# Four transformer layers on one core: the third layer's sliding-block units gathered into two runs of four, and into one run of eight for the last chunk

## The chip, the core and the metric

The kernel runs on one core of one Trainium2 chip. The metric is the device time of one execution in microseconds (us). A core has five engines that run side by side and meet through semaphores: TensorE (PE in the profile, its weight loads PEld) multiplies matrices, ScalarE (ACT) computes exponentials, VectorE (DVE) and GpSimd (POOL) do elementwise work, and SyncE (SP) issues DMA transfers. ACT, POOL and SP also have a queue of their own for issuing transfers; what stands in a queue is issued in order.

## The reference: what is computed

The input x has 2048 rows of 640 numbers. Four attention layers follow one another, and each adds its result to x:

```python
x = A_x
x = x + _A_ref(_layernorm(x, axis=-1), A_wqkv, A_wo)
x = x + _B_ref(_layernorm(x, axis=-1), B_wqkv, B_wo)
x = x + _A_ref(_layernorm(x, axis=-1), A_wqkv, A_wo)
x = x + _B_ref(_layernorm(x, axis=-1), B_wqkv, B_wo)
```

Both kinds have 32 heads of 20 numbers: queries, keys and values come from one product with wqkv, scores are q·k/sqrt(20), softmax over the keys, the weighted sum of the values, and a product with wo. In `_A_ref` a query sees itself and the 255 keys before it (a sliding block); in `_B_ref` it sees all 2048 keys. The kernel numbers the layers 0 to 3, so that 0 and 2 are sliding ("windowed" in the code) and 1 and 3 are full. The change concerns layer 2, the third layer.

## The kernel before

**Chunks, groups, units.** The rows are cut into 4 chunks of 512 queries and the heads into 8 groups of 4. The attention of one layer, one chunk and one group is a *unit*, `Unit(l, c, g)`; below it is written l.c.g. A full unit has 64 *banks* (16 blocks of 128 keys by 4 heads; one bank is a 128 x 512 block of scores in PSUM), a windowed unit has 12. Layer 3's chunk 0 is done in two parts, over key blocks 0 to 11 (48 banks) and, later, 12 to 15 (16 banks), because its last keys are ready late.

**Tiles.** The banks of all units stand in one list in the order of `units` and are cut into *tiles* of three banks (some of two). For each tile PE computes the scores (line 1316, two halves of three or four of the eight PSUM banks), ACT takes the exponential of the whole tile in one instruction (line 1347, into a tile `pt` of 6 buffers), and two or three tiles later PE multiplies by the values (line 1380). A tile of a windowed unit is masked in between: `affine_select` on POOL (line 1419) and a product with a mask on DVE (line 1429); its product with the values waits for both. In a full unit of layer 1 two of the 64 banks are "aside": their exponential is made on DVE (line 918 and following), and their scores sit in two tiles whose ACT instruction has two banks. So a layer-1 unit of chunk 1 to 3 has 21 or 22 tiles, a windowed unit 4, and a first part in layer 3 has 16.

**Background work.** The chain between two layers has to go on while these tiles run: when all 8 units of (l, c) have ended and been divided by their softmax sums (the *tails*, lines 1020 to 1090, one for two units that ended one after the other, about 8 tiles long), the output projection `t_out` is queued (work 9.0), and with it, for the same chunk of the next layer, the layer norm `t_ln` (1.6), the values `t_v` (5.6) and ten blocks `t_block` of 128 features, one for keys and one for queries (1.1 each; `qk`, line 536 stores the block to DRAM, line 337 loads its weights, both from the POOL queue). A windowed unit g then loads its rows of q and k from DRAM on the SP queue (lines 770 and 771). Each of these tasks uses a bank of PSUM, number 6, that all of them share.

**Due times set the pace.** A task is due when the first unit that needs it starts. Between two tiles `pump` gives the background an amount `rate(t)`:

```python
        def rate(t):
...
            done, r = 0.0, 0.6 if state["early"] else 0.3
            for task in todo:
                done += max(task.left, 0.0)
                if task.need < len(units):
                    r = max(r, done / max(starts[id(units[task.need])] - t - 16, 1))
            return min(1.1 * r, 1.0 if u.l == 0 else 0.9)
```

`starts` holds the tile with which a unit starts; the work is meant to be over 16 tiles ahead, the amount per tile is at least 0.33 and at most 0.9, and what isn't done when the unit starts is done there and then (`require`). If a tile has little background work, `keep_clock` adds matmuls whose result nobody reads (`unread`, in the profile `ps<-masks,ident`), so that PE stays busy.

**Where the change is.** The order of `units` is written out by hand. Behind each unit g of layer 1's chunk c (c = 1, 2, 3), and for c = 4 behind each first part of layer 3's chunk 0, a tuple says how many of layer 2's eight units of chunk c - 1 follow. Before, they stand in pairs behind the units g = 2, 3, 4 and 5, and for the last chunk two, three and three behind g = 2, 3 and 4. The starts by tile follow from the bank counts: 2.0.0 starts at tile 413, 2.1.0 at 616, 2.2.0 at 819, 2.3.0 at 1005; the last units of the four chunks end at tiles 509, 712, 915 and 1069. Layer 3's first parts start at tile 957, its second parts at 1117, and layer 3's chunk 1 at 1160.

Of the kernel before, what the change touches and what calls it, by code (L numbers as in the profile page):

```python
# [26 lines left out]
NC = S // C  # L27
# [21 lines left out]
def kernel(  # L49
# [689 lines left out]
    for c in range(1, NC + 1):  # L739
        small = deque(Unit(2, c - 1, g) for g in range(G))  # L740
        for g in range(G):
            units.append(Unit(1, c, g) if c < NC else Unit(3, 0, g, PARTS[3][0]))
            for _ in range(((0, 0, 2, 2, 2, 2, 0, 0) if c < NC else (0, 0, 2, 3, 3, 0, 0, 0))[g]):
                units.append(small.popleft())
    units += [Unit(3, 0, g, PARTS[3][1]) for g in range(G)]
    units += [Unit(3, c, g) for c in range(1, NC) for g in range(G)]
# [730 lines left out]
```

## Time and profile before

| | |
|---|---|
| median of 3 runs | 2251.73 us (2251.3 to 2252.52) |
| the profiled execution | 2252.22 us, its span 2250.5 us |
| ACT busy | 2147.6 us, 95% of the span, 1734 instructions |
| of these line 1347, the exponentials | 2110.4 us, 1656 instructions |
| PE busy | 1959.8 us (87%) |
| DVE busy | 1201.6 us (53%) |
| POOL busy | 485.4 us (22%) |
| granted TensorE clock, mean | 0.989 |

The profiled execution took 1.7 us more than its span (start and end, outside the trace) and 0.5 us more than the median of the runs. In the profile "L1347" is line 1347 of the kernel, `pt<-ps` an instruction that reads the tile `ps` and writes `pt`, and a time behind "<-" is idle time of an engine and what ended it. A stretch A:B of the trace runs from A to B us after the span's start. Some positions, read from the starts of ACT's exponentials: tile 349 (unit 1.1.0) at 493.0 us, 413 at 580.6, 552 (unit 1.2.0) at 755.8, 616 at 845.2, 755 (unit 1.3.0) at 1030.9, 819 at 1124.1, 957 at 1310.8, 1005 at 1383.4, 1117 at 1537.6, 1160 at 1595.1.

### The profile page before, as it was taken

To read this page: it belongs to the slowest core of one execution; us is meant where nothing else is said; L and a number is where in the kernel's file an instruction comes from. 1 tells how busy PE (TensorE), PEld (TensorE's weight loads), DVE (VectorE), ACT (ScalarE), POOL (GpSimd) and SP (SyncE) were. 2 spreads that over 40 slices of the span, in tenths; PEclk is the share of its full clock that TensorE was granted. 3 is DMA by queue.
4 is the path that set the end of the run, shared out by engine and by line. 5 is a ranking of instruction groups with operands and counts; after the bars stand their busy time and mean duration, and the time that the engine had idled before them with its cause. 6 is when DMAs were issued, how large, how long until landed. Compare 5 with 4: busy or idle time off the path is not lost.

```text
span 2250.5 us, 71088 instructions
## 1 busy us (share of the span) xinstructions
PE 1959.8 (87%) x30915; PEld 773.2 (34%) x30915; DVE 1201.6 (53%) x2178; ACT 2147.6 (95%) x1734; POOL 485.4 (22%) x950
## 2 busy tenths in 40 slices
PE   8989899988888888888888888888888888888888
PEld 4444443334333343333333443343332222222222
DVE  6656564435343554345453533242567767767774
ACT  7899899999999999999899999999999999999997
POOL 6664544201111124111331123212000000000000
PEclk9999999999999999999999999999999999999999
DMA  6233322422110233012320033103111111111100
GB/s 197 73 98 89 92 79 86 106 71 65 58 35 21 62 100 89 15 35 58 95 84 15 23 105 105 29 22 92 58 59 31 31 34 40 31 31 37 43 25 16
DMA packets 88408, 137.15 MB, mean 61 GB/s; under 512 B 20766, under 2 KB 63486, under 8 KB 88094
## 3 DMA queue, kind: packets, MB, share of 16 engines
q1 hardware_dynamic: 68878, 79.43, 12.7%
q0 software_dynamic: 19216, 53.17, 8.1%
q8 instruction: 242, 3.96, 0.7%
q14 instruction: 72, 0.59, 0.1%
HBM read 99.52 MB, written 27.79 MB: 57 GB/s over the span
## 4 chain that ended last, share of the span: by engine, by line
ACT 47%; PE 26%; issue 16%; DVE 9%; POOL 1%; DMA 1%; SPq 1%; ACTq 0%; DVEq 0%; POOLq 0%
ACT pt L1347 46%; PE ps L300 16%; PE ps L1316 6%; PE ps L1380 2%; DVE st L323 1%; DVE x_sb L568 1%; DVE on L1090 1%; DVE va L323 1%; DVE pt L1429 1%; PE ps L1086 1%; DVE vs L323 0%; DVE raw_o L934 0%; PE ps L437 0%; DVE xnT L323 0%; SPq L1103 0%
## 5 line engine op out<-in xcount | busy, mean ns | idle before, releaser
L1347 ACT ACTIVATE pt<-ps 128x1536 bf16<-128x1536 f32 (+2 forms) x1656 | 2110.4, 1448 | 70.4 <-PE ps L1316 58.0
L300 PE MATMUL ps<-masks,ident 128*32 128x512 bf16 x6344 | 549.7, 390 | 101.3 <-ACT pt L1347 58.2
L1316 PE MATMUL ps<-qt,kt 32*128 32x512 bf16 x3960 | 549.5, 386 | 88.8 <-ACT pt L1347 80.6
L1380 PE MATMUL ps<-pt,vt 128*21 128x512 bf16 x3904 | 397.9, 383 | 0.3 <-ACT pt L1347 0.2
L1316 PEld LDWEIGHTS <-kt 32*128 32x128 bf16 x3960 | 163.7, 91 | 551.2 <-issue 536.4
L1419 POOL TENSOR_SCALAR_AFFINE_SELECT pt<-pt 128x256 bf16<-128x256 bf16 (+2 forms) x505 | 215.8, 448 | 376.5 <-ACT pt L1347 339.4
L300 PEld LDWEIGHTS <-ident 128*32 128x32 bf16 x6344 | 165.5, 94 | 342.6 <-issue 332.0
L300 PE MATMUL ps<-xnT,wqk 128*32 128x512 bf16 x3320 | 221.6, 384 | 16.4 <-DVE st L323 7.9
L1429 DVE TENSOR_TENSOR pt<-pt,masks 128x512 bf16<-128x512 bf16 (+4 forms) x267 | 114.0, 439 | 190.0 <-ACT pt L1347 188.2
L323 DVE CAST st<-ps 128x512 bf16<-128x512 f32 x134 | 92.7, 692 | 210.8 <-PE ps L300 210.7
L300 PE MATMUL ps<-wop,on 128*32 128x320 bf16 x3712 | 157.7, 302 | 17.1 <-DMA on<-on 6.3
L918 DVE TENSOR_SCALAR xnT<-ps 128x512 int32<-128x512 f32 x136 | 93.6, 688 | 134.7 <-PE ps L912 123.6
L1380 PEld LDWEIGHTS <-vt 128*21 128x21 bf16 x3912 | 105.6, 91 | 129.2 <-issue 90.7
L1316 PE MATMUL ps<-qa,ka 32*128 32x384 bf16 (+2 forms) x1408 | 118.7, 278 | 32.2 <-ACT pt L1347 29.6
L300 PEld LDWEIGHTS <-on 128*32 128x32 bf16 x5760 | 116.8, 95 | 80.6 <-issue 58.3
L568 DVE TENSOR_TENSOR x_sb<-x_sb,ps 128x320 bf16<-128x320 bf16 x120 | 58.3, 486 | 125.0 <-PE ps L300 124.7
L1090 DVE TENSOR_TENSOR on<-on,ps 128x512 bf16<-128x512 bf16 x128 | 86.4, 684 | 68.6 <-PE ps L1086 66.6
L300 PE MATMUL ps<-wv,xnT 128*32 128x320 bf16 x2560 | 112.5, 301 | 10.2 <-DVE on L1090 2.2
L300 PEld LDWEIGHTS <-wqk 128*32 128x32 bf16 x3320 | 79.9, 96 | 111.6 <-issue 58.8
L864 DVE CAST on<-ps 128x512 bf16<-128x512 f32 x112 | 77.0, 688 | 69.9 <-PE ps L1389 38.1
L934 DVE SCALAR_TENSOR_TENSOR xnT<-xnT 128x1024 f32<-128x1024 f32 x68 | 83.3, 1225 | 2.3
L1316 PEld LDWEIGHTS <-ka 32*128 32x128 bf16 x1408 | 43.6, 92 | 116.3 <-issue 109.1
(100 smaller groups left out, 1468.2 us busy)
## 6 DMA issues: line engine op xcount, KB each, us to landing
vt<-v_d SPq DMA_DIRECT2D x48, 336.0 KB
kt<-k_d SPq DMA_DIRECT2D x192, 80.0 KB
wqk<-in_B_wqkv_dram POOLq DMA_DIRECT2D x80, 160.0 KB, 3.5
wqk<-in_A_wqkv_dram POOLq DMA_DIRECT2D x70, 160.0 KB, 3.5
k_d<-st POOLq DMA_DIRECT2D x75, 128.0 KB, 2.4
q_d<-st POOLq DMA_DIRECT2D x75, 128.0 KB, 2.3
qt<-q_d SPq DMA_DIRECT2D x384, 20.0 KB
v_d<-vs POOLq DMA_DIRECT2D x16, 336.0 KB, 3.5
```

Of the source, the lines that this page charges most:

```text
L300: nc.tensor.matmul(out_[r], lhsT=lhsT[:, r], rhs=rhs, start=start, stop=stop)
L323: nc.vector.tensor_copy(out=out_, in_=in_)
L568: nc.vector.tensor_tensor(out=xv, in0=had, in1=yp, op=ALU.add)
L864: nc.vector.tensor_copy(out=oT, in_=op)
L918: V.tensor_scalar(out=xi.bitcast(I32)[:, i * C : (i + 1) * C], in0=side["psum"], scalar1=SCALE * LOG2E * FIX, scalar2=-127.0 * FIX, op0=AL ...
L934: V.scalar_tensor_tensor(out=xi, in0=xm, scalar=EA, in1=xm, op0=ALU.add, op1=ALU.mult)
L1090: nc.vector.tensor_tensor(out=oT, in0=oT, in1=zb, op=ALU.mult)
L1316: nc.tensor.matmul(sp[:, i, col * P : (col + qn) * P], lhsT=u.k(kc, j), rhs=u.q(j, q0, qn), start=True, stop=True,)
L1347: nc.scalar.activation(out=pt[:, i:k, b0 * P :], in_=sp[:, i:k, b0 * P :], func=ACT.Exp, scale=SCALE,)
L1380: nc.tensor.matmul(op[32 * j : 32 * j + VW, q0 * P : (q0 + qn) * P], lhsT=u.v(kc, j), rhs=pg[:, i, col * P : (col + qn) * P], start=(first ...
L1419: nc.gpsimd.affine_select(out=v, in_=v, compare_op=ALU.is_gt if later else ALU.is_ge, fill=0.0, base=0, pattern=[[0, k - i], [-1 if later ...
L1429: nc.vector.tensor_tensor(out=pt_[:, i:k, cols], in0=pt_[:, i:k, cols], in1=mv_, op=ALU.mult)
```

## The change

One line changes. In chunks c = 1 to 3 the eight units of layer 2 come as four behind unit 1.c.3 and four behind 1.c.4; in the last, all eight behind the first part of 3.0.3. Nothing is added to or taken from the units themselves.

```diff
         for g in range(G):
             units.append(Unit(1, c, g) if c < NC else Unit(3, 0, g, PARTS[3][0]))
-            for _ in range(((0, 0, 2, 2, 2, 2, 0, 0) if c < NC else (0, 0, 2, 3, 3, 0, 0, 0))[g]):
+            for _ in range(((0, 0, 0, 4, 4, 0, 0, 0) if c < NC else (0, 0, 0, 8, 0, 0, 0, 0))[g]):
                 units.append(small.popleft())
```

With the same bank counts the starts become: 2.0.0 at tile 435, 2.1.0 at 637, 2.2.0 at 840, 2.3.0 at 1021; the last windowed units end at tiles 488, 691, 893 and 1053. Every other landmark stays (552, 755, 957, 1117, 1160).

## The prediction

> **What bounds the kernel.** I read the page first, then the waits of ACT, then ACT's exponentials by stretch.
>
> ```profile
> PE 1959.8 (87%) x30915; PEld 773.2 (34%) x30915; DVE 1201.6 (53%) x2178; ACT 2147.6 (95%) x1734; POOL 485.4 (22%) x950
> ...
> L1347 ACT ACTIVATE pt<-ps 128x1536 bf16<-128x1536 f32 (+2 forms) x1656 | 2110.4, 1448 | 70.4 <-PE ps L1316 58.0
> ```
>
> ACT is the bound, and its exponentials are 2110 of its 2148 us; when it idles, it is for PE's scores (58.0 of 70.4 us). The change leaves every exponential as it is: with the bank counts I get 1161 tiles up to unit 3.1.0 and the same number of ACT instructions in both orders, and 240 selects and 128 mask products for layer 2 in both. So only the waiting can change. Where it stands, the stretches show (us, ACT busy and instructions, granted clock, DMA share, GB/s):
>
> ```profile
> 493.00:580.60 87.60, 85.05 (x65) 1.00 0.28 73
> 755.80:857.90 102.10, 96.44 (x74) 0.99 0.29 83
> 1030.90:1124.10 93.20, 85.77 (x66) 0.98 0.25 72
> 1250.60:1310.80 60.20, 56.75 (x44) 1.00 0.21 56
> 1310.80:1383.40 72.60, 66.85 (x50) 1.00 0.37 100
> 1469.00:1537.60 68.60, 65.52 (x50) 1.00 0.20 53
> 1124.10:1250.60 126.50, 126.29 (x97) 1.00 0.15 46
> 1383.40:1469.00 85.60, 85.60 (x66) 1.00 0.16 48
> 1415.30:1431.20 15.90, 15.90 (x13) 1.00 0.22 61
> ```
>
> The last row is twelve tiles of three consecutive windowed units without a gap: 15.9/12 = 1.33 us a tile, the bare pitch. Successive starts of two-bank tiles without a wait are 0.90 us apart. A stretch is *late* by its length less 1.33 and 0.90 for each of its tiles (busy time hides part of this, since a record of ACT gets longer when the next instruction isn't there):
>
> - A, 493.0 (tiles 349 to 413, before layer 2's chunk 0): 58 x 1.33 + 6 x 0.90 = 82.5; late 5.1
> - B, 755.8 (552 to 624, before and into chunk 1): 93.2; late 8.9
> - C, 1030.9 (755 to 819, before chunk 2): 82.5; late 10.7
> - D, 1250.6 (915 to 957, from chunk 2's last unit to layer 3): 54.1; late 6.1
> - E, 1310.8 (957 to 1005, before chunk 3): 63.8; late 8.8
> - F, 1469.0 (1069 to 1117, from chunk 3's last unit to the second parts): 63.8; late 4.8
> - the calm stretches between, 1124.1 and 1383.4: late 1.4 and 0.5.
>
> Together 44 us, and all of it lies just before a due time. The tasks' own rows say why (projection matmuls of `wqk` in C, before the due time, and in a calm stretch as long as one unit):
>
> ```profile
> 1086.80:1124.10 37.30, 15.73 (x224) 6.24 (x224) 0.00 (x0) 7.32 (x9) 0.95 0.34 105
> 1134.70:1162.00 27.30, 7.63 (x104) 2.38 (x104) 0.00 (x0) 2.59 (x3) 1.00 0.23 68
> ```
>
> The first has 224 of them in 22 tiles and is late by 8.9 us; the second 104 in 21 tiles and late by 0.2. Ten a tile make PE late with the scores, five fit.
>
> **The change, part by part.** *More time before the due times.* The work due with the first windowed unit is 9.0 + 1.6 + 5.6 + 2.2 = 18.4. The projection that starts it (`ps<-wop,on`) begins at 506.8, 773.6, 1048.5, 1264.7, 1328.8 and 1485.1 us: tiles 359, 565, 768, 925, 970 and 1080. By `rate` that is, as 1.1 x 18.4/(due - start - 16), with due tile before and after:
>
> - A: 413, then 435: 0.53 to 0.34
> - B: 616, then 637: 0.58 to 0.36
> - C: 819, then 840: 0.58 to 0.38
> - D: due 957 in both, but the last unit ends 22 tiles earlier; it now makes a tail of its own, some 5 tiles, so start 905 or so: 0.9 (the cap) to 0.56
> - E: 1005, then 1021: 0.9 to 0.58
> - F: due 1117, start 16 tiles earlier, 1064: 0.9 to 0.55
>
> A rate of 0.36 is the calm stretch's (floor 0.33). What is late at 0.58 B and C show: through output projection and layer norm 1.3 and 1.8 us; only behind that, when the 16 tiles of margin are used up and the rate climbs to 0.9, 7.5 and 8.9. So I take for after: A 3.0 (bursts of the layer norm and of the start, 1.8, stay), B 1.5, C 1.8 (calm level), D 2.0 (of its blocks only b = 0 is due at 957, the next 16 tiles later), E 4.5 (the output projection's 3.5 go to 0.6, its blocks stay like B's), F 1.7. Saved: 2.1 + 7.4 + 8.9 + 4.1 + 4.3 + 3.1 = 29.9 us. Bounds: nothing (if a burst is as large at any rate) and 37 (all at the calm level, some 1.2 each).
>
> *Longer runs of windowed tiles.* Runs grow from 8 and 12 tiles to 16 and 32. The load of one such tile shows in the twelve of 1415.3:
>
> ```profile
> 850.50:857.90 7.40, 5.86 (x82) 1.95 (x74) 4.38 (x7) 5.74 (x6) 6.77 (x14) 0.80 0.65 185
> ...
> 1104.10:1107.50 3.40, 3.40 (x31) 1.12 (x34) 1.02 (x2) 1.43 (x1) 0.03 (x1) 0.50 0.00 0
> 1415.30:1431.20 15.90, 12.34 (x215) 5.09 (x214) 6.47 (x13) 15.90 (x13) 9.60 (x20) 1.00 0.22 61
> ```
>
> (columns: PE, PEld, DVE, ACT, POOL busy). POOL is busy 60%, DVE 41%, PE 78%, and no time is lost. But 850.5, unit 2.1.1, shows what happens when a block falls among them: POOL issues two weight loads (1.73 us) and a store (0.56) ahead of the selects, PE waits for masks, ACT for PE, and four tiles take 7.35 instead of 5.32, 2.03 us late (part of it at a halved clock, below). A block costs POOL 0.87 + 0.57 = 1.44 us. In A to C the blocks are now over before the run or nearly; in E those due at tiles 1033 to 1045 (three pairs) can fall into the run. I take two such incidents, 4.1 us; ends: none (as at 1415.3), and one in each unit that has windowed units before it in its run, 6 x 3 + 7 = 25, 51 us.
>
> *Loads and queues.* SP issues 8 loads for each windowed unit, some 0.3 us each, 2.4 us in 5.3; four units can be ahead (`QA`), so the fifth is loaded three units, 16 us, before its use; POOL's stores land 2.3 us after issue. Waits of PE on these transfers are 4 us in all now. I cost it at nothing; if this cover went, the price is of the size of those 4 us. *One tail more* in each of c = 1 to 3 (an odd unit): 16 tiny matmuls and some 0.35 + 0.21 + 0.20 + 0.21 us on DVE, beside a DVE at half load: nothing. The unread matmuls fill whatever tasks leave, so PE's total hardly moves.
>
> *The clock.* At 1104.1 and 854.9 the granted clock was 0.50 for 3.4 us; twenty matmuls took 2.33 us there, 1.29 elsewhere, and the tile at 1104.1 came 2.1 us late. The twelve windowed tiles kept 1.00. I add nothing. The Trainium skill ("TensorE: Matmul & The Clock Gate", "HAM oscillation — how this bites in real kernels") speaks against long thin stretches: idle gaps of PE over about 3.4 us halve its clock. By that rule, once in each of the seven runs at the 2.1 us seen, the sum would be 15 us worse, 2241; the trace shows no such gap in a run. The skill also has POOL and DVE share SBUF interfaces when DVE reads two SBUF inputs ("GPSIMD Engine Reference", "Specifications"), as the masks do; but the same pairs meet in both orders.
>
> **Sum.** 2252.2 (the profiled execution) - 29.9 + 4.1 = 2226.4; its 0.5 us over the median I subtract: 2226.
>
> **Rivals.**
> 1. *The late due times gain nothing*: D, E and F go from the cap to 0.56, near B's rate, and B is as late as E. Then 18.4 us (A to C) are saved, 4.1 lost: 2238. Against it: in D to F half of the loss stands at the output projection, which at B's rate cost 1.3. Chance 0.16.
> 2. *All becomes calm* and the runs cost nothing: 2252 - 37 = 2215. Against it: E's rate isn't calm. Chance 0.11.
> 3. *The work only moves*: the same bursts, bound to the one shared bank and not to the pace, stand in other tiles: 2252. Against it: the 104 matmuls of the calm stretch. Chance 0.06.
> 4. *Slower: POOL in the runs.* Masks, stores and weight loads share one in-order queue; if tasks (layer 3's too) keep running in the runs and each of the 25 units is late as 2.1.1 was: 2252 - 30 + 51 = 2273. It decides from 15 such units on. For it: 850.5; against: 1415.3, and that the work is over sooner. Chance 0.05.
>
> My forecast, 2226 (2217 to 2236), gets 0.62. The range 2214 to 2241 takes in rivals 1 and 2 to their own small spread and leaves out 3 and 4. A measurement of this kernel can tell about 0.2%, 4.5 us, from no change: faster 0.62 + 0.16 + 0.11 = 0.89, same 0.06, slower 0.05.
>
> **What would show it.** Right: stretches B and C fall to 1 to 2 us late, D and F lose their bursts of 28 and more `wop` matmuls a tile, ACT's wait for scores falls from 58 us to some 42 (the six stretches hold 28 us of ACT's idle time for their 44 us of lateness), windowed runs keep 1.33. Wrong: "ACT waits for POOL" (4.4 us now) grows; the blocks of `wqk` still come ten a tile before tiles 637 and 840; halved clocks inside the runs.

## The result, and the profile after

The changed kernel takes 2230.31 us (median of 4 runs, 2229.77 to 2231.19), the kernel before 2252.12 in the same comparison: ratio 0.9906, 95% interval 0.9894 to 0.9918, that is 21 us or 0.94% faster. 2226 was forecast, range 2214 to 2241. The profiled execution took 2229.77 us, its span 2228.1.

The page's line of the exponentials, then the rows of ACT's waits for scores and for masks:

```profile
L1347 ACT ACTIVATE pt<-ps 128x1536 bf16<-128x1536 f32 (+2 forms) x1656 | 2104.2, 1456 | 55.4 <-PE ps L1316 45.7
```

```profile
ACT pt L1347 <- PE ps L1316: 45.7, 71, 3.2
...
ACT pt L1347 <- POOL pt L1419: 2.7, 2, 2.2
```

Still 1656 exponentials; ACT waits 45.7 us for scores in place of 58.0 (42 was forecast), and less for POOL than before (2.7, was 4.4). The same six stretches, found again from the starts of ACT's exponentials (us, ACT busy and instructions, clock, DMA share, GB/s):

```profile
494.20:578.20 84.00, 83.73 (x66) 1.00 0.19 48
755.50:850.00 94.50, 93.94 (x74) 1.00 0.29 79
1024.20:1109.50 85.30, 84.44 (x66) 1.00 0.25 69
1240.60:1298.80 58.20, 55.01 (x44) 0.97 0.26 73
1298.80:1363.70 64.90, 64.89 (x49) 1.00 0.26 72
1451.60:1516.40 64.80, 64.39 (x49) 1.00 0.26 71
```

A comes down from 87.6 to 84.0 us, B from 102.1 to 94.5, C from 93.2 to 85.3, D from 60.2 to 58.2, E from 72.6 to 64.9 and F from 68.6 to 64.8. As lateness (length less 1.33 us for each tile of three banks and 0.90 for each of two), in the kernels that are compared most below:

| | A | B | C | D | E | F | A to F | 624-755 | 819-915 | 1005-1069 |
|---|---|---|---|---|---|---|---|---|---|---|
| before | 5.1 | 8.9 | 10.7 | 6.0 | 8.7 | 4.7 | 44.1 | 3.1 | 1.4 | 0.5 |
| after | 1.4 | 2.2 | 2.7 | 4.1 | 1.1 | 1.0 | 12.5 | 3.5 | 6.0 | 2.7 |
| late start only | 1.4 | 4.7 | 1.5 | 6.8 | 2.1 | 4.7 | 21.3 | 4.7 | 6.3 | 2.4 |
| early end only | 6.4 | 5.6 | 9.0 | 3.4 | 6.3 | 0.2 | 30.9 | 2.5 | 3.3 | 1.6 |
| after, old pace | 6.8 | 4.8 | 9.4 | 4.5 | 5.4 | 2.7 | 33.6 | 2.1 | 4.8 | 2.6 |
| before, no margin | 0.9 | 22.8 | 10.5 | 11.2 | 8.6 | 6.5 | 60.5 | 3.4 | 14.5 | 11.1 |
| before, margin of 8 | 1.8 | 5.5 | 6.2 | 7.6 | 8.3 | 6.2 | 35.6 | 3.5 | 2.6 | 0.3 |
| one run of eight | 1.1 | 4.0 | 3.3 | 0.4 | 1.1 | 0.3 | 10.1 | 2.2 | 2.2 | 2.7 |

The last three columns are the calm stretches between, named by their tiles. The six stretches give 31.6 us. What comes back is 9: 4.6 us in tiles 819 to 915, 2.2 in 1005 to 1069, 2.1 in tiles 413 to 552 (the stretch with chunk 0's windowed units, not in the table) and 0.4 in 624 to 755; 1.9 us more are lost ahead of tile 349, where both kernels are the same. Seven profiled kernels of this study have the same code up to that tile, and it took them 474.9 to 481.0 us from the first exponential on: a single profile's total is good to a few us only, so totals below are medians and single stretches are read from profiles. One execution of the study, the first of the late start below, took 8681 us and is left out: its matmuls took about four times as long (the unread ones 1543 ns in the mean, 390 before) at a recorded clock of 1.00, while the exponentials took 1362 ns (1448 before).

The tasks answer to the rows of the prediction (projection matmuls of `wqk` just before chunk 2's due tile; columns PE, PEld, DVE, POOL busy):

```profile
1080.00:1109.50 29.50, 2.17 (x36) 0.69 (x28) 0.00 (x0) 2.29 (x3) 1.00 0.20 57
...
1109.50:1138.50 29.00, 10.36 (x144) 3.15 (x140) 0.00 (x0) 5.20 (x6) 1.00 0.41 119
```

36 of these matmuls stand in the 22 tiles of unit 1.3.2 where 224 stood before; 144 stand in the unit behind it (second row), at some seven a tile, and that unit is 0.6 us late. Unit 1.3.2 took 37.3 us and takes 29.5.

### The profile page after: what moved, and what is told of

Its sections match the earlier page's. It is cut to its first block, busy times and chain, and to the rows that moved or that the text cites. A ratio compares the mean times of both kernels' runs of the same rounds, so it can differ in the third digit from the quotient of the medians.

```text
span 2228.1 us, 70079 instructions
## 1 busy us (share of the span) xinstructions
PE 1933.2 (87%) x30410; PEld 757.7 (34%) x30411; DVE 1200.5 (54%) x2190; ACT 2141.2 (96%) x1734; POOL 484.0 (22%) x950
## 3 DMA queue, kind: packets, MB, share of 16 engines
q1 hardware_dynamic: 68878, 79.43, 12.8%
## 4 chain that ended last, share of the span: by engine, by line
ACT 51%; PE 22%; issue 17%; DVE 7%; DMA 1%; POOL 1%; SPq 0%; ACTq 0%; DVEq 0%; POOLq 0%
ACT pt L1347 50%; PE ps L300 13%; PE ps L1316 6%; PE ps L1380 2%; DVE on L1090 1%; DVE st L323 1%; DVE pt L1429 1%; DMA wqk<-in_B_wqkv_dram 1%; PE ps L1086 1%; PE ps L437 0%; DVE x_sb L568 0%; DVE on L864 0%; SPq L1103 0%; DVE raw_o L918 0%; DVE xnT L323 0%
## 5 line engine op out<-in xcount | busy, mean ns | idle before, releaser
L1347 ACT ACTIVATE pt<-ps 128x1536 bf16<-128x1536 f32 (+2 forms) x1656 | 2104.2, 1456 | 55.4 <-PE ps L1316 45.7
L300 PE MATMUL ps<-masks,ident 128*32 128x512 bf16 x5840 | 513.8, 389 | 118.3 <-ACT pt L1347 68.4
L1429 DVE TENSOR_TENSOR pt<-pt,masks 128x512 bf16<-128x512 bf16 (+4 forms) x267 | 112.9, 438 | 96.7 <-ACT pt L1347 94.5
L536 POOL DMA_DIRECT2D k_d<-st x75 | 43.0, 574 | 236.8 <-DVE st L323 226.9
```

The source lines that it names most:

```text
L300: nc.tensor.matmul(out_[r], lhsT=lhsT[:, r], rhs=rhs, start=start, stop=stop)
L536: nc.gpsimd.dma_start(out=dst, in_=staging.pop())
L1347: nc.scalar.activation(out=pt[:, i:k, b0 * P :], in_=sp[:, i:k, b0 * P :], func=ACT.Exp, scale=SCALE,)
L1429: nc.vector.tensor_tensor(out=pt_[:, i:k, cols], in0=pt_[:, i:k, cols], in1=mv_, op=ALU.mult)
```

## The experiments

The theory: background work that is due soon is issued at a pace that makes PE late with the scores; the change gives it more tiles. The rivals: longer runs of windowed units save something by themselves; or only the early end matters. The edits are shown against the changed kernel, in the two runs of the old order against the kernel before.

**Late start only.** Runs start as after, end as before.

```diff
-            for _ in range(((0, 0, 0, 4, 4, 0, 0, 0) if c < NC else (0, 0, 0, 8, 0, 0, 0, 0))[g]):
+            for _ in range(((0, 0, 0, 4, 2, 2, 0, 0) if c < NC else (0, 0, 0, 5, 3, 0, 0, 0))[g]):
```

> Layer 2's runs start where the changed kernel starts them (behind the fourth unit) and end where the kernel before ends them: (0,0,0,4,2,2,0,0), last chunk (0,0,0,5,3,0,0,0). Theory, time before the due times: stretches A, B, C and E (the work due with the first windowed unit) keep their saving of 3.7 + 5.4 + 7.9 + 7.6 us in the changed kernel's trace, D and F (due with layer 3) lose theirs, 1.9 + 3.7: 2230 + 6 = 2236 us. Rival, the length of the runs: half of the runs are as long as after, so about 2241. Rival, the early end is what saves: 2248 or more.

Measured: 2238.2 us in the mean of four executions, ratio 0.9939 (0.9920 to 0.9958), 14 us faster than before. The stretches come from a second profile:

> Another profile of the late start alone, whose time was 2238 us. By the theory of the due times its stretches A, B, C and E are as little late as in the changed kernel (1.4, 1.5, 2.7, 1.1 us) and D and F as late as in the kernel before (6.0 and 4.7).

A, C, D and F in that profile:

```profile
494.40:578.30 83.90, 83.63 (x65) 1.00 0.19 48
1027.20:1111.30 84.10, 83.88 (x66) 1.00 0.18 47
1242.70:1303.60 60.90, 56.78 (x43) 1.00 0.21 56
1457.10:1525.70 68.60, 65.53 (x49) 1.00 0.21 53
```

A and C are as short as in the changed kernel (84.0, 85.3), D and F as long as in the kernel before (60.2, 68.6). The two halves of the change act where their due times lie, as the theory has it; E (2.1) nearly does, and only B (4.7) is between.

**Early end only.** Runs start as before, end as after.

```diff
-            for _ in range(((0, 0, 0, 4, 4, 0, 0, 0) if c < NC else (0, 0, 0, 8, 0, 0, 0, 0))[g]):
+            for _ in range(((0, 0, 2, 2, 4, 0, 0, 0) if c < NC else (0, 0, 2, 6, 0, 0, 0, 0))[g]):
```

> The runs start where the kernel before starts them and end where the changed kernel ends them: (0,0,2,2,4,0,0,0), last chunk (0,0,2,6,0,0,0,0). Theory: only D and F gain, 1.9 + 3.7 us: about 2246 us, and A, B, C and E are as late as before (5, 9, 11, 9 us). Rival, the length of the runs: about 2241. Rival, the early end is what saves: 2232.

Measured: 2244.1 us, ratio 0.9962 (0.9949 to 0.9975), 8.5 us faster. D and F come down to 3.4 and 0.2; A (6.4) and C (9.0) stay; B (5.6) and E (6.3) come down in part, which the theory doesn't say. 13.7 and 8.5 us add up to the 21 of the whole change, so there is no saving that needs both. That the runs are longer can't be the reason by itself: here they are about as long as in the late start, and the saving stands elsewhere.

**The changed order at the old pace.**

```diff
+        def sooner(u):
+
+            if u.l == 2 and u.g < 2:
+                return 22 if u.c < NC - 1 else 16
+            if u.l == 3 and u.c == 0:
+                return 20 if u.part == PARTS[3][0] else 16
+            return 0
...
-                    r = max(r, done / max(starts[id(units[task.need])] - t - 16, 1))
+                    r = max(r, done / max(starts[id(units[task.need])] - sooner(units[task.need]) - t - 16, 1))
```

> The changed order of units, but the pace of the background reckoned as if the units were due when the kernel before had them: 22 tiles sooner for the first two windowed units of chunks 0 to 2, 16 sooner for chunk 3, 20 and 16 sooner for layer 3's two parts. The order on ACT is that of the changed kernel. Theory, the pace makes PE late: the lateness of A to F comes back, some 20 to 28 us: 2250 to 2258. Rival, the order of the units itself (longer runs, fewer changes between masked and unmasked tiles) saves: 2230.

Measured: 2245.2 us, ratio 0.9970 (0.9957 to 0.9984). With every unit where the change puts it, 15 of the 21 us are gone. A is at 6.8, C at 9.4 us again:

```profile
491.00:580.30 89.30, 85.31 (x65) 0.98 0.28 72
1026.70:1118.60 91.90, 85.56 (x65) 0.98 0.33 91
```

This is the test that carries the most: the order was kept and the loss came back. In the six stretches 21.1 us did (33.6 against 12.5), within the 20 to 28 expected; of C's 9.4, 3.2 are one tile (805) in which PE waited 1.2 us for weights and the clock then halved. The total rose by less: in this profile the part ahead of tile 349, the same code, took 4.0 us less than in the changed kernel's, and the stretches between the six 3.6 less. Part of the old 44.1 can't come back: the 2 us of tiles 621 and 623, where blocks fell among the masks of unit 2.1.1, need a windowed unit at that place.

**The old order at a slower pace.** If the pace is all, it could be slowed without moving a unit, by letting the tasks end at the due tile and not 16 tiles ahead.

```diff
-                    r = max(r, done / max(starts[id(units[task.need])] - t - 16, 1))
+                    r = max(r, done / max(starts[id(units[task.need])] - t, 1))
```

> The order of the kernel before, but the pace is reckoned to the due tile itself and not to 16 tiles ahead of it. Rates by the formula: 0.37, 0.40, 0.40 before chunks 0 to 2, 0.63, 0.58 and 0.55 before layer 3, chunk 3 and the second parts, close to those of the changed kernel (0.34, 0.36, 0.38, 0.56, 0.58, 0.55). Theory: most of the 22 us comes without any change of order, 2230 to 2238, less what is finished in a hurry when a unit starts. Rival, the order itself: 2252.

Measured: 2311.9 us, ratio 1.0268 (1.0248 to 1.0288): 60 us slower. The chain between tiles 615 and 616, where chunk 1's first windowed unit is due (start, us, what), shows what the 16 tiles are for:

```profile
849.70 1.29 PE ps L300 x20
851.01 0.70 DVE st L323
...
851.75 1.29 PE ps L300 x20
853.07 0.70 DVE st L323
853.77 0.28 issue
854.05 2.42 DMA q_d<-st
856.49 0.27 SPq L770
...
856.86 0.28 SPq L771
...
857.19 1.63 DMA qa<-q_d
...
858.87 0.73 PE ps L1316 x3
```

From the last projection's end at 853.0 to the scores at 858.9 that wait for it the block goes through DVE, a store to DRAM (2.42 us), SP's queue and a load (1.63), 5.8 us in all, with two projections back to back ahead of it; the tile is 8.5 us late. It happens at each first need: 6.9 us in chunk 0, 8.5 and 8.1 before units 2.1.0 and 2.1.1, 9.2 and 9.0 in chunk 2, 4.8 and 4.5 in chunk 3, 6.9 and 5.2 at layer 3's two due times. My expectation left this way out. What the pace does without it shows when these tiles are taken off: A to F are then 0.9, 6.2, 1.4, 4.3, 3.8 and 1.4 us late, 18 us for the 44 before, with no unit moved. The same with half of the margin:

```diff
-                    r = max(r, done / max(starts[id(units[task.need])] - t - 16, 1))
+                    r = max(r, done / max(starts[id(units[task.need])] - t - 8, 1))
```

> The order of the kernel before, the pace reckoned to 8 tiles (10.6 us) ahead of the due tile in place of 16. The run without any margin lost 8 to 9 us at each unit that needed its blocks at once, so 8 tiles should just hold the way through DRAM. Rates by the formula: 0.45, 0.47, 0.47 before chunks 0 to 2 and 0.84, 0.75, 0.70 later, between those of the kernel before and those of the changed one. Theory, the pace makes PE late: 2238 to 2246, faster than before with no unit moved. Rival, the order itself must change: 2252, or slower where the margin is too short.

Measured: 2248.7 us, ratio 0.9985 (0.9974 to 0.9996), faster by 1 to 6 us: less than expected. A to F fall to 35.6; A, B and C improve as their rates do, D to F, whose rates stay at 0.7 to 0.84, don't (22.1 us late, 19.5 before; 2.8 of it in tile 1113, where PE waits for weights). The edit also changes the pace ahead of tile 349, and in this profile that part took 483.5 us, 6.5 more than before, so the total isn't the price of the six stretches alone. So the pace can be eased in the old order too, but with neither of the two margins did the total come near what the units' places give.

**Where 9 us came back.** Behind the first run of four, units 1.2.4 and 1.3.4 are 2.1 and 4.0 us late (0.6 each before). DVE at that place, first column the start:

```profile
894.26 0.68 DVE L918 TENSOR_SCALAR raw_o<-ps 128x512 int32<-128x512 f32 x1
894.86 0.67 DVE L1090 TENSOR_TENSOR on<-on,ps 128x512 bf16<-128x512 bf16 x1
895.46 0.68 DVE L923 TENSOR_SCALAR raw_o<-raw_o 128x1024 f32<-128x1024 uint16 x1
896.06 0.68 DVE L929 TENSOR_SCALAR raw_o<-raw_o 128x1024 int16<-128x1024 int16 x1
896.66 0.68 DVE L1090 TENSOR_TENSOR on<-on,ps 128x512 bf16<-128x512 bf16 x1
897.26 1.21 DVE L934 SCALAR_TENSOR_TENSOR raw_o<-raw_o 128x1024 f32<-128x1024 f32 x1
```

and PE's waits for it:

```profile
895.59 0.40 PE L300 MATMUL ps<-masks,ident 128*32 128x512 bf16 x4 [0.85 <-DVE on L1090]
...
897.39 0.40 PE L300 MATMUL ps<-masks,ident 128*32 128x512 bf16 x4 [0.43 <-DVE on L1090]
```

The tails of the run's units (line 1090 reads the shared bank) come just when unit 1.2.4 starts its side exponentials (918 to 946). DVE has no gap, the tail's products stand among the side operations, and PE, whose next matmul goes into the bank that the product reads, waits 0.85 and 0.43 us. Then the clock halves (last section). Before, this unit began at the same tile, with another tail at another moment. First suspect were the unread matmuls:

```diff
-            if mfree[b][0] > state["tick"] - (0 if state["early"] else 0):
+            if mfree[b][0] > state["tick"] - (0 if state["early"] else 1):
```

> The changed kernel, but an unread matmul goes into the shared bank only when the bank has been free for a tile more, else into the next tile's score banks. Theory on the new loss behind the first run of four (1.2.4 2.1 us, 1.3.4 4.0 us late): the unread matmul waits there for DVE's product of a tail, PE sits idle within its windows, and the clock halves. Then those two units fall below 1 us and the total is 2224 to 2228. Rival, the DVE side work and tails as such make the tiles late: 2230, and the two units stay at 2 and 4.

Measured: 2228.7 us, ratio 0.9898 (0.9879 to 0.9917), not told apart from the changed kernel, and the two units stay at 2.1 and 3.8. The theory isn't settled by this: in this run's trace the same unread matmuls wait 0.85 and 0.43 us at the same place. They come with the tails' own next steps (`warm_bank`, lines 1083 and 1044), which the edited line of `keep_clock` doesn't reach. So the bank itself was held back a tile longer:

```diff
-    def drop_m(b):
+    def drop_m(b, more=0):
...
-        mfree[b] = (state["tick"] + (not state["early"]), mseq[0])
+        mfree[b] = (state["tick"] + (not state["early"]) + more, mseq[0])
...
         nc.vector.tensor_tensor(out=oT, in0=oT, in1=zb, op=ALU.mult)
-        drop_m(mb)
+        drop_m(mb, int(not state["early"]))
```

> The changed kernel, but the shared bank that a tail's product reads (line 1090) is given to the next task one tile later, so that PE meets the wait for DVE a tile later. The run with later unread matmuls left units 1.2.4 and 1.3.4 at 2.1 and 3.8 us, so the wait is that of the bank's next user, whoever it is, for a product that stands behind side work on DVE. If so, the two units fall below 1 and 1.5 us and the total to 2223 to 2228. Rival, the tiles are late because DVE as such is full there: 2230, the lateness moves to the score tiles or to the values' product.

Measured: 2234.4 us, ratio 0.9916 (0.9902 to 0.9931). Unit 1.2.4 falls from 2.1 to 0.9 us, PE's two waits and the half clock behind them are gone, so there the bank's wait was the cause. 1.3.4 only falls to 3.4, late now at its first tiles, and B, which is not near, rises to 7.2: 2.7 us of that are one tile (593), in which PE waits 3.4 us for a copy on DVE that stands behind a step of the layer norm on POOL. In sum nothing is won. That DVE's side work and the tails collide is shown in 1.2.4; how much of the 9 us it makes isn't settled. The clock has a part in it: in the run with the longer lead, below, which leaves the bank as it is, the clock doesn't halve in 1.3.4 and the unit is 1.8 us late, where in the changed kernel it is at half for 6.8 us and 4.0 late.

**The one tile of D.** Tile 942 is 3.3 us late of D's 4.1. PE's weight load and POOL's queue there:

```profile
1276.75 0.14 PEld L300 LDWEIGHTS <-wqk 128*32 128x32 bf16 x8 [1.84 <-DMA wqk<-in_B_wqkv_dram]
```

```profile
1269.40 0.82 POOL L494 DMA_DIRECT2D v_d<-vs  x1 [16.70 <-DVE vs L323]
1270.94 0.75 POOL L494 DMA_DIRECT2D v_d<-vs  x1 [0.72 <-issue]
1271.69 1.73 POOL L337 DMA_DIRECT2D wqk<-in_B_wqkv_dram  x2
```

The weights are issued behind the two stores of the values, which waited for DVE; the planner counts them as there 4 tiles after they are queued.

```diff
-        wtick[l, n, c, i] = state["tick"] + 4
+        wtick[l, n, c, i] = state["tick"] + 6
```

> The changed kernel, but a block's weights are counted as landed 6 tiles after their load was written into POOL's queue, not 4. In the changed kernel's stretch D (4.1 us late, 2.0 forecast) tile 942 alone is 3.3 us late: PE waits for weights whose load stood in POOL's queue behind two stores of values. Theory, the lead of 4 tiles (5.3 us) is too short behind those stores: tile 942 comes on time, D falls to about 1 us, the total to 2226 to 2229. Rival, the half clock in that place is what costs: D stays at 3 to 4 and the total at 2230.

Measured: tile 942 comes in 1.33 us, D is 1.9 us late. That the wait for weights starts the delay is shown. It isn't all of the 3.3 us: in the run with later unread matmuls, which keeps the 4 tiles, the load of weights waits as long, but the clock stays at 1.00 and the tile is 1.7 us late, so the half clock costs the other 1.6.

```profile
1275.07 0.34 PEld L300 LDWEIGHTS <-wqk 128*32 128x32 bf16 x12 [1.77 <-DMA wqk<-in_B_wqkv_dram]
```

The total, 2231.7 us, ratio 0.9915 (0.9896 to 0.9934), is the changed kernel's: what 2 us here are worth can't be told from the spread of the runs.

**More of the same.** Runs of chunks 0 and 1 a unit later, and one run of eight everywhere:

```diff
-            for _ in range(((0, 0, 0, 4, 4, 0, 0, 0) if c < NC else (0, 0, 0, 8, 0, 0, 0, 0))[g]):
+            for _ in range(((0, 0, 0, 4, 4, 0, 0, 0) if c == NC - 1 else (0, 0, 0, 0, 4, 4, 0, 0) if c < NC else (0, 0, 0, 8, 0, 0, 0, 0))[g]):
```

> The runs of four of chunks 0 and 1 one unit later, behind the fifth and sixth unit: (0,0,0,0,4,4,0,0); chunks 2 and 3 as in the changed kernel. The rate before chunks 0 and 1 is at its floor, 0.33, either way. Theory, once the rate is at the floor more time gives nothing: 2228 to 2231. Rival, each unit of delay brings more: 2225 or less.

Measured: 2226.0 us (2221.0 to 2231.1), ratio 0.9884 (0.9859 to 0.9908). A and B are as late as in the changed kernel (1.4, 2.2), C 1.5: at the floor of the rate there is no more to get there. The 4 us under the changed kernel lie within the runs' spread.

```diff
-            for _ in range(((0, 0, 0, 4, 4, 0, 0, 0) if c < NC else (0, 0, 0, 8, 0, 0, 0, 0))[g]):
+            for _ in range(((0, 0, 0, 8, 0, 0, 0, 0) if c < NC else (0, 0, 0, 8, 0, 0, 0, 0))[g]):
```

> All eight units of every chunk in one run behind the fourth unit: (0,0,0,8,0,0,0,0). The starts are those of the changed kernel, the last unit ends 22 tiles sooner in chunks 0 to 2, so the rate before layer 3 (D) falls from 0.56 to 0.36. Theory: D loses its bursts, about 1 us, and the loss behind the first run moves behind the only run: 2227 to 2231. Rival 4 of the prediction, POOL in long runs: each of the units in the run late by 2 us, 2260 or more.

Measured: 2222.5 us, ratio 0.9864 (0.9843 to 0.9886), the lowest median of the study, against 0.9906 (0.9894 to 0.9918) for the change: faster than both kernels. D falls to 0.4 us late, F to 0.3, and tiles 819 to 915 from 6.0 to 2.2. Behind the run of chunk 1 the tail's two products stand at 918.0 and 919.5 us, ahead of the block of side operations from 920.7, and units 1.2.4 and 1.3.4 are 1.2 us late each, without a half clock. D and F:

```profile
1241.00:1295.60 54.60, 54.60 (x44) 1.00 0.21 62
...
1448.30:1512.40 64.10, 64.10 (x49) 1.00 0.27 71
```

ACT has no idle time left in them. The rival of the long runs (2260) is out. With the tail's bank held longer as well (both edits above):

> One run of eight in every chunk, and the tail's bank given on one tile later. The single run alone gave 2222.5 us and had no such loss behind its runs (2.2 and 2.0 us late from tile 640 to 755 and 819 to 893). If the bank's wait is what the later release takes away, little is left to gain here: 2219 to 2223. Rival, tails that take a tile longer hold the chain up: 2225 or more.

Measured: 2223.2 us, ratio 0.9869 (0.9852 to 0.9886): no further gain.

## Why the prediction was right, and where it wasn't

*What bounds, and where the loss stands*: right. ACT's work didn't change, the lateness before the due times fell from 44 to 12.5 us. *The pace as the cause*: right for most of it; the old pace alone takes back 15 of the 21 us, and 21.1 of the 31.6 in the six stretches.

*More time before the due times, 29.9 us*: measured 31.6. Term by term, forecast and measured lateness after: A 3.0 and 1.4, B 1.5 and 2.2, C 1.8 and 2.7, D 2.0 and 4.1, E 4.5 and 1.1, F 1.7 and 1.0. (For C the formula gives a rate of 0.36, not 0.38.) Two were mis-sized. E: I let its blocks stay as late as B's, since the rate is the same 0.58; but B and C were late where the margin was used up and the rate had climbed: C's last 16 tiles before had 12.8 projection matmuls of `wqk` a tile. The due tile of E moved to 1021, and the last 16 tiles ahead of it now have 8.5 a tile and are 1.3 us late; with them E is 2.4 late, not 4.5. D: 3.3 of its 4.1 us are one late load of weights and the half clock behind it, which the run with the longer lead removes.

*Longer runs, 4.1 us for two incidents of POOL*: this step failed. The run of eight lost 0.2 us in its 32 tiles (42.7 us for 32 times 1.33), the first runs of four in chunks 1 and 2 0.4 and 0.2 us in 16 (columns PE, PEld, DVE, ACT, POOL busy):

```profile
867.30:888.90 21.60, 17.56 (x365) 7.99 (x361) 13.24 (x29) 21.60 (x17) 14.14 (x32) 1.00 0.30 90
...
1137.20:1158.60 21.40, 17.54 (x368) 8.07 (x364) 13.30 (x30) 21.40 (x17) 14.69 (x34) 1.00 0.29 85
...
1386.30:1429.00 42.70, 35.50 (x701) 15.49 (x698) 24.96 (x55) 42.70 (x34) 29.45 (x63) 1.00 0.14 41
```

In the run of eight (last row) POOL is busy 69% (29.45 us), DVE 58%, and ACT never waits. All but the last of its blocks were over before it (20 `wqk` matmuls stand in it). But that isn't the whole reason: in the two runs of four, 80 and 76 `wqk` matmuls stand among the masks, POOL issues one load of weights and three or four stores of blocks in each, and ACT has no idle time there either. So the price of 2.03 us that I took from unit 2.1.1 was itself too high. What came back, 9 us, came from outside the runs: behind the first run of four, in the calm stretch of the last chunk (where its remaining blocks and an output projection now stand), and in the stretch of chunk 0's windowed units. I had costed the tails at nothing beside a DVE at half load; on average it is, but in the three tiles where side work and tails meet it is full. That the total came within 4 us of 2226 is luck in part: the 4.1 us for the runs, which weren't lost there, stand in for some of the 9 that were lost elsewhere, and the stretches gave 1.7 more than forecast.

*Loads, queues*: nothing, as costed, in the runs: the 4 us that I named as the price were waits for the full units' `qt`, and those for the windowed units' `qa` and `ka` were 1.3 us before and are 1.1. But loads of weights behind a store in POOL's queue cost 1.7 us in D, 3.3 with the half clock. *The clock*: no half clock inside the runs, as taken; but two behind the runs of four and one in D, for a reason that I didn't know (below). Of the rivals, 1 is out (D to F fell from 19.5 to 6.2 us), 3 is out (the matmuls that moved behind stand there with 0.6 us of lateness), 4 is out. 2 missed the total, 2215, though it was right that the runs cost next to nothing.

## What to carry to other kernels

When the bounding engine loses its time in bursts just ahead of due times, moving the consumer later can win most of them back, with none of the work made cheaper: look at which work is due, how many tiles it has, and at what pace the feeding engine still keeps up. Keep the margin that covers the way through DRAM (here 5 to 9 us at a first need) out of that bargain. And look behind the moved block for the engine that is idle on average and full for a few tiles; a last test that groups even more is cheap and had the lowest median here.

## What the runs showed of the hardware that wasn't expected

The clock of TensorE halves without a long idle gap. In the changed kernel (PE, PEld, DVE, ACT, POOL busy, granted clock behind them):

```profile
894.50:897.90 3.40, 2.12 (x59) 1.11 (x55) 3.40 (x6) 2.63 (x3) 0.11 (x1) 0.99 0.11 39
897.90:901.30 3.40, 3.40 (x39) 0.67 (x30) 1.31 (x5) 2.74 (x3) 0.00 (x0) 0.50 0.02 5
1273.30:1276.70 3.40, 1.91 (x54) 0.65 (x46) 3.30 (x7) 3.40 (x3) 2.45 (x4) 1.00 0.87 249
1276.70:1280.10 3.40, 3.35 (x31) 1.02 (x33) 1.34 (x2) 0.29 (x1) 0.00 (x0) 0.51 0.33 97
```

PE was busy 2.12 and 1.91 of 3.4 us, its longest gaps 0.85 and 1.5 us, and the next 3.4 us ran at half clock. The changes of the clock lie on a grid of 3.41 us. Cut 13 profiles (both kernels and eleven runs) on that grid, from 400 us on, and sort the windows at full clock by PE's busy share in them, as the profile models the ends of matmuls: of 34 below 0.5 all 34 were followed by a window at half clock, of 38 between 0.5 and 0.6 18, of 152 between 0.6 and 0.7 7, of 6641 above 5. At only 9 of these 64 does PE have an idle gap of 3.4 us or more. So a few waits of under a microsecond each, falling into one window, can cost 1 to 2 us more than themselves (1.6 in tile 942). The grid doesn't start with the kernel, so the same code can meet it differently in each execution: of the seven profiles with the same code up to tile 349, the shortest (474.9 us) was at half clock there for 3.4 us, the two longest (481.0) for 23.9 and 27.3. The Trainium skill ("TensorE: Matmul & The Clock Gate", "HAM oscillation — how this bites in real kernels") has the rule as idle gaps of more than about 3.4 us; these runs show it as a busy share of one window, mostly with shorter gaps.
